# Linear attention and an MLP mixer in one kernel: the last batch's outputs sent in 16 transfers of two queues, not 24

## The chip, the core and the metric

The kernel runs on one core of a Trainium2 chip. The metric is the device time of one execution in microseconds (us); the time before is the median of three runs. One more execution was taken by the hardware profiler, and the profile's views come from it.

## The reference

For 8 batches, 8 heads of 64 columns and 576 rows (float32 in and out), the reference computes a linear attention and feeds it to a mixer:

```python
q_p, k_p = phi(q), phi(k)                      # phi(x) = elu(x) + 1
kv  = einsum('bhsd,bhse->bhde', k_p, v)
num = einsum('bhsd,bhde->bhse', q_p, kv)
den = einsum('bhsd,bhd->bhs', q_p, k_p.sum(axis=2))[..., None] + 1e-06
x   = (num / den), laid out as (8, 576, 512)
h   = relu(x.transpose(0, 2, 1) @ w_tok1) @ w_tok2   # 576 -> 256 -> 576, mixes the rows
u   = x + h.transpose(0, 2, 1)
out = u + relu(u @ w_ch1) @ w_ch2                    # 512 -> 1536 -> 512
```

## The kernel before

The 576 rows of a batch lie as 64 groups of 9. Eight of the nine rows of each group are packed in pairs into four row tiles of 128 partitions: in a tile, partitions 0 to 63 hold one row of each group and partitions 64 to 127 the next one. The ninth rows ("tails") of two batches share a tile of their own. Matmuls run in bf16, sums in float32 PSUM.

Every piece of work is a named step, registered with `put(name, function, arguments)`. The string `ORDER` is a hand-written list of step names, and the kernel issues the steps in exactly that order. Each engine and each queue works through its own part of the list in order, and a step waits on semaphores for the data that it needs. A name begins with the batch, so 7... is the last batch. The steps that matter here:

- `7p<i><j>` (`product`, L959), i = 1 to 7, j = 0 or 1: the seven products of a Strassen-Winograd scheme for the last matmul, `relu(...) @ w_ch2`, of the row tiles 2j and 2j+1. Each is six matmuls of 128x256 into a PSUM bank.
- `7R<i><j>` (`product_read`, L973): VectorE (DVE) adds product i to one 256-column half of a row tile in the float32 buffer `obuf`. Each half of a row tile gets two such additions; the one with the later place in `ORDER` completes it. Products 1 and 2 make tile d = 0, columns 0 to 255; 6 and 3 the same tile's columns 256 to 511; 5 and 7 tile d = 1, columns 256 to 511, with 4 for its columns 0 to 255, which build on the same bank.
- `7D<i><j><e>` (`product_put`, L978): a DMA of one finished column half of one partition half (e) of a row tile to HBM: 64 rows of 256 float32, 64 KB. It is sent by SyncE (SP) for e = 0 and by ScalarE (ACT) for e = 1. ScalarE has no computation left at that time.
- `7ta<i>`, `7tb<i>`, `7t<i>` (`tail_product`, L1012), `7tr<i>` (`tail_read`, L1019), `7td<i><b>` (`tail_put`, L1024): the same for the tails of batches 4 to 7, two tiles of 128 rows; again SP sends partitions 0 to 63 and ACT partitions 64 to 127.

So the last batch's output and the four tails leave in 2 (j) x 4 (halves of two tiles) x 2 (e) = 16 transfers of L978 and 4 x 2 = 8 of L1024, 12 on each of the two queues. The outputs of the earlier batches leave through GpSimd (POOL) (`pair_put`, L1062, two transfers of 512 KB a batch), and nothing else is sent in the last microseconds. The program has eight completion semaphores for the transfers of SP and ACT and uses them in turn, so a transfer also waits until the eighth before it has landed. After the last step SP waits for all transfers to land (L1180), and a barrier of all engines ends the program.

Of the kernel before, what the change touches and what calls it, by code (L numbers as in the profile page):

```python
# [16 lines left out]

NO = 6

GSW = {2: 0, 1: 1}  # L20

HOLD = {2: 'p0 p1 p2', 1: 's2 s3 s2'}
# [5 lines left out]
ON_DVE = {'1v0', '2v1', '0r3', '0r6', '0r9', '1r5', '1r8'}  # L28

ON_POOL = set()  # L30

BANK = {k_: int(v_) for k_, v_ in (e.split(":") for e in """2K:5 2n0:2 2n1:4 2n2:6 2f:2 2g0:5 2g1:2 2X2:7 2Z2:0 2Y2:2 2gt:6 3K:6 3n0:2 3n1:4 3n2:6 3f:3 3g0:2 3g1:4 3X2:1
3Z2:5 3Y2:6 3gt:6 4K:2 4n0:2 4n1:4 4n2:6 4f:4 4g0:3 4g1:6 4X2:1 4Z2:4 4Y2:3 4gt:6 5K:3 5n0:2 5n1:4 5n2:6 5f:5
# [61 lines left out]
7y02 7y06 6p70 7y16 7x07 7y15 6eW 7x22 7y21 7x25 6hW 7y22 6p41 7y25 7x17 7F4 W1 7x26 7c2 7s4 7y26 7y17 7x23  # L95
7cr2 7x03 7x14 7y03 7x27 7y14 7y23 6p40 7y07 7x13 7c0 7w30 6eX 7c3 7y27 6o 7x04 7x12 7y04 7x24 7y12 7cr0 7c4
7cr3 7y13 7y24 7p10 7w34 7cr4 7w12 7p11 7w10 7w22 7c1 7w14 7w24 7p50 7R10 7cr1 7w20 7c5 7w40 7w42 7p60 7w32
7cr5 7w44 7ta2 7ts1 7R60 7ta1 7tb1 7p70 7tr1 7R11 7p21 7ts2 7R50 7p61 7R21 7R70 7p30 7D701 7ts4 7tb2 7p40 7p20
7R40 7R30 7t6 7D401 7ts3 7tr2 7D300 7R61 7D211 7p51 7tr6 7D700 7R20 7D301 7t5 7td20 7R51 7D201 7p71 7D210 7tr5
7td21 7t7 7D200 7R71 7D400 7t3 7D711 7tr7 7D710 7p31 7td71 7tr3 7td70 7p41 7td31 7R31 7td30 7t4 7D311 7R41  # L100
7D310 7D411 7tr4 7D410 7td41 7td40"""


@with_exitstack
def kernel(
# [20 lines left out]
    nc = tc.nc  # L126

    B, H, S, D = q.shape
# [3 lines left out]
    R = 4  # L132
    R1 = R + 1
    T = 2 * R + 1
    TD = T * D
# [14 lines left out]
    def bank(name):  # L150
        return psum[:, BANK[name]]
# [11 lines left out]
    def const(name, shape, dt=BF16):  # L163
        return consts.tile(shape, dt, name=name, tag=name)
# [18 lines left out]
    ut = [const(f"ut{i}", [128, DM]) for i in range(2)]  # L183
    uT = [const(f"uT{b}", [128, R, NDM, 128]) for b in range(2)]
    uTj = [t.rearrange("p r j c -> p (r j c)").rearrange("p (j r c) -> p j r c", j=NDM, r=R) for t in uT]
    ebuf = [const(f"e{i}", [128, 2 * TD]) for i in range(4)]
    ybuf = [const(f"y{i}", [128, 2 * TD]) for i in range(2)]
    uTt = const("uTt", [128, 2, NDM, 128])
    cr = [const(f"cr{b}", [128, NCH, SM]) for b in range(2)]
    crt = const("crt", [128, NCH, 128])  # L190
    obuf = const("obuf", [128, NO, DM], FP32)
    swc = const("swc", [128, len(GSW), 4, 2, 256])

# [5 lines left out]
    half = [slice(0, 64), slice(64, 128)]  # L199
# [27 lines left out]
    def put(name, fn, *a):  # L227
        assert name not in tok, name
        tok[name] = lambda: fn(*a)
# [4 lines left out]
    def slots(name, m):  # L234
        return obuf[:, SLOT[name]:SLOT[name] + m]
# [120 lines left out]
            in0=v_[:, :, :, 0:D],  # L356
            in1=den[:, :, :, None].to_broadcast([128, m, HG, D]), op=ALU.mult)

    for i in range(3):
        for c in range(2):  # L360
            put(f"1n{i}{c}", nd1_mm, i, c)
            put(f"1nc{i}{c}", nd1_end, i, c)
# [49 lines left out]
            out=xv[:, :, 3, m], in0=nd_tile(n, m)[:, :, at, 0:D],  # L412
            in1=dens[:, m, :, at, None].to_broadcast([128, 2, D]), op=ALU.mult)

    for n in range(2, B):
        put(f"{n}n", nd_mm, n)
        put(f"{n}nd", nd_den, n)
        put(f"{n}ne", nd_last, n)
        for m in range(3):
            put(f"{n}n{m}", nd_six, n, m)  # L420
        for m in range(2):
            put(f"{n}o{m}", nd_one, n, m)
# [62 lines left out]
    for n in range(1, B):  # L485
        for mt in range(NT):
            put(f"{n}f{mt}", mm1, n, mt)
            put(f"{n}fr{mt}", mm1_read, n, mt)
        if n > 1:
            for i in range(2):  # L490
                put(f"{n}g{i}", mm2, n, i)
                put(f"{n}gu{i}", mm2_read, n, i)
                put(f"{n}uT{i}", utr_dma, n, i)
        if n > 1 and n % 2:
            put(f"{n}gt", mm2_tails, n // 2)
            for b in range(2):
                put(f"{n}gt{b}", mm2_tails_read, n // 2, b)
            put(f"{n}ut", utr_tail_dma, n // 2)
# [173 lines left out]
    def mm3(n, mc, kjs):  # L672
        b = n % 2
        for kj in kjs:
            nc.tensor.matmul(out=bank(f"{n}m{mc}"), lhsT=wc1[:, kj, 128 * mc:128 * mc + 128],  # L675
                             rhs=uTj[b][:, kj] if n < 2 else uT[b][:, :, kj],
                             start=(kj == 0), stop=(kj == NDM - 1))

    def mm3_read(n, mc):
# [6 lines left out]
    for n in range(B - 1):  # L686
        for mc in range(NCH):
            if n < 2:
                put(f"{n}ma{mc}", mm3, n, mc, range(0, 2))
                put(f"{n}mb{mc}", mm3, n, mc, range(2, NDM))  # L690
            else:
                put(f"{n}m{mc}", mm3, n, mc, range(NDM))
            put(f"{n}r{mc}", mm3_read, n, mc)
# [47 lines left out]
    outv = out.rearrange("n (p t) d -> n p t d", t=T)  # L741
# [76 lines left out]
    def ablock(n, i, e):  # L818
        return cr[n % 2].rearrange("p k (j e s) -> p k j e s", j=2, e=2)[:, KH * i:KH * (i + 1), :, e]
# [7 lines left out]
    def row_sums(n, which, k0, m):  # L827
        live["row", n, which, k0] = winograd(
            sb, [ablock(n, i, e) for e in range(2) for i in range(2)], which, slice(k0, k0 + m),
            nc.gpsimd if f"{n}w{which}{k0}" in ON_POOL else nc.vector)  # L830

# [15 lines left out]
    def cblock(m, h):  # L847
        return wc1[:, 2 * h:2 * h + 2, HM * m:HM * (m + 1)]
# [21 lines left out]
    def u_sums(n, which):  # L870
        t, b = tu if n == B - 1 else tuc, n % 2
        b11, b12, b21, b22 = [ublock(h, e, b) for h in range(2) for e in range(2)]
        x_, y_ = {1: (b12, b11), 2: (b22, t[0]), 3: (b22, b12), 4: (b21, t[1])}[which]
        (nc.gpsimd if f"{n}s{which}" in ON_POOL else nc.vector).tensor_tensor(
            out=t[which - 1], in0=x_, in1=y_, op=ALU.subtract)

    for n in range(2, B):
        for w in range(1, 5):
            put(f"{n}s{w}", u_sums, n, w)

    def group_sums(g, which):
        s_ = swc[:, GSW[g]]
        a11, a12, a21, a22 = [cblock(m, h)[:, :, 256 * g:256 * g + 256] for m in range(2) for h in range(2)]
        o, x_, y_, op = ((0, a21, a22, ALU.add), (1, s_[:, 0], a11, ALU.subtract),
                         (2, a11, a21, ALU.subtract), (3, a12, s_[:, 1], ALU.subtract))[which - 1]
        (nc.gpsimd if f"G{g}{which}" in ON_POOL else nc.vector).tensor_tensor(
            out=s_[:, o], in0=x_, in1=y_, op=op)

    for g in GSW:
        for w in range(1, 5):  # L890
# [11 lines left out]
    def mix_mm(n, g, i):  # L902
# [5 lines left out]
        else:  # L908
            s_, t, c0 = [swc[:, GSW[g], w] for w in range(4)], tuc, 0
        w_ = lambda m, h: cblock(m, h)[:, :, 256 * g:]  # L910
# [23 lines left out]
            o, c = {2: (dst(0, 0), c1), 3: (dst(0, 1), c6), 7: (dst(1, 1), c5)}[i]  # L934
            add_relu(o, ps, c)

    for n in range(2, B):
        for g in range(3) if n == B - 1 else GSW:
            for i in range(1, 8):
                put(f"{n}x{g}{i}", mix_mm, n, g, i)  # L940
                put(f"{n}y{g}{i}", mix_read, n, g, i)
# [21 lines left out]
    HC = [slice(0, 256), slice(256, 512)]  # L963
# [11 lines left out]
    def product_put(n, i, j, e):  # L975
        o = slots(f"{n}P{j}", 2)
        d, c = {2: (0, 0), 7: (1, 1), 3: (0, 1), 4: (1, 0)}[i]
        [nc.sync, nc.scalar][e].dma_start(out=outv[n, :, 2 * (2 * j + d) + e, HC[c]],  # L978
                                          in_=o[half[e], d, HC[c]])

    for n in range(1, B):
        for i in range(1, 8):
# [2 lines left out]
    for i in range(1, 8):  # L985
        for j in range(2):
            put(f"7R{i}{j}", product_read, 7, i, j)
            for e in range(2):
                if i in (2, 3, 4, 7):
                    put(f"7D{i}{j}{e}", product_put, 7, i, j, e)  # L990


# [28 lines left out]

    def tail_put(i, b):
        e, c = {2: (0, 0), 7: (1, 1), 3: (0, 1), 4: (1, 0)}[i]
        (nc.sync, nc.scalar)[b].dma_start(out=outv[B - 4 + 2 * e + b, :, 2 * R, HC[c]],  # L1024
                                          in_=slots("7t", 2)[half[b], e, HC[c]])

    for w in range(1, 5):
        put(f"7ts{w}", tail_sums, w)
    for i in range(1, 8):
        if i < 3:  # L1030
            put(f"7ta{i}", tail_product, i, range(KH - 1))
            put(f"7tb{i}", tail_product, i, range(KH - 1, KH))
        else:
            put(f"7t{i}", tail_product, i, range(KH))
        put(f"7tr{i}", tail_read, i)
        for b in range(2):
            if i in (2, 7, 3, 4):
                put(f"7td{i}{b}", tail_put, i, b)


# [144 lines left out]
```

## Time and profile before

| | |
|---|---|
| median of 3 runs | 248.88 us (248.19 to 249.03) |
| profiled execution | 248.42 us; span from first to last instruction 246.6 us; granted TensorE clock 0.997 |
| PE busy | 235.1 us (95%), 2538 matmuls |
| DVE busy | 204.1 us (83%) |
| ACT busy | 136.9 us (56%) |
| POOL busy | 78.7 us (32%) |
| output transfers of SP and ACT | 12 + 12 of 64.0 KB, 2.1 us to landing (median) |
| HBM read, written | 35.85 MB, 9.44 MB |

Engines are PE (TensorE matmul), DVE (VectorE), ACT (ScalarE), POOL (GpSimd) and SP (SyncE). An engine name with a q (ACTq, SPq) stands for its queue, and what it issues (a DMA) is not counted as busy time. L978 is line 978 of the kernel before. A DMA's duration in the timeline is that of its issue on the queue; the time to landing counts from the start of the issue until the last piece has arrived.

### The profile page before, as it was taken

What the parts mean: (1) busy time and instruction counts of PE and PEld (TensorE: products, weight loads), DVE (VectorE), ACT (ScalarE), POOL (GpSimd) and SP (SyncE); (2) the same over time, 40 slices, a digit from 0 to 9 for tenths busy, and PEclk for the clock granted to TensorE, in tenths of its full rate; (3) what the DMA queues carried; (4) which work ended last, traced back from release to release, by engine and by line L of the source; (5) the groups of instructions that cost most, each with busy time, mean ns of one, the idle gap of its engine ahead of it and who ended that gap; (6) DMA issues with size and microseconds to landing.
All of it is one profiled execution on the core that took longest, in us unless ns stands there. A gap on an engine that the chain in (4) does not pass through costs nothing.

```text
span 246.6 us, 6211 instructions
## 1 busy us (share of the span) xinstructions
PE 235.1 (95%) x2538; PEld 168.5 (68%) x2556; DVE 204.1 (83%) x368; ACT 136.9 (56%) x224; POOL 78.7 (32%) x88
## 2 busy tenths in 40 slices
PE   7899999999999999999999999999999999999990
PEld 3584445565776676777777676867687758888880
DVE  5954686999899899998996989889997789687670
ACT  4761882579684298429957378448822742535000
POOL 9770047071900440062000260044006700532730
PEclk9999999999999999999999999999999999999998
DMA  6999999988879996399939984599375434126145
GB/s 251 266 203 253 362 239 290 387 235 206 318 210 204 304 335 167 77 262 334 351 104 204 313 273 99 104 190 295 77 160 24 88 85 88 21 45 142 35 115 139
DMA packets 50445, 48.42 MB, mean 196 GB/s; under 512 B 30192, under 2 KB 36720, under 8 KB 50416
## 3 DMA queue, kind: packets, MB, share of 16 engines
q1 hardware_dynamic: 41984, 35.00, 49.9%
q0 software_dynamic: 7472, 12.22, 23.9%
q10 hardware_dynamic: 960, 0.79, 1.4%
q8 instruction: 20, 0.33, 0.5%
q14 instruction: 9, 0.07, 0.1%
HBM read 35.85 MB, written 9.44 MB: 184 GB/s over the span
## 4 chain that ended last, share of the span: by engine, by line
PE 88%; DVE 3%; DMA 3%; issue 2%; ACT 2%; DVEq 0%; SPq 0%; ACTq 0%
PE ps L959 24%; PE ps L917 16%; PE ps L675 15%; PE ps L437 6%; PE ps L736 6%; PE ps L448 4%; PE ps L700 2%; PE ps L722 2%; PE ps L291 2%; PE ps L1012 2%; PE ps L376 2%; DMA k_raw<-in_k_dram 2%; DMA qT<-qp 1%; PE ps L309 1%; PE ps L616 1%
## 5 line engine op out<-in xcount | busy, mean ns | idle before, releaser
L675 PE MATMUL ps<-uT,wc 128*128 128x512 bf16 x171 | 40.9, 379 | 0.2
L684 ACT ACTIVATE cr<-ps 128x512 bf16<-128x512 f32 x39 | 22.4, 600 | 23.3 <-PE ps L675 18.1
L1058 POOL TENSOR_TENSOR obuf<-obuf,q_raw 128x512 f32<-128x512 f32 x6 | 8.8, 1465 | 72.0 <-DVE obuf L1051 72.0
L959 PE MATMUL ps<-k_raw,v_raw 128*128 128x256 bf16 x252 | 31.6, 273 | 0.0
L675 PEld LDWEIGHTS <-wc 128*128 128x128 bf16 x176 | 16.7, 98 | 16.7 <-issue 0.2
L959 PEld LDWEIGHTS <-cr 128*128 128x128 bf16 x252 | 24.3, 98 | 5.0 <-issue 0.4
L959 PEld LDWEIGHTS <-v_raw 128*128 128x128 bf16 x252 | 24.3, 98 | 3.9 <-issue 0.4
L241 ACT ACTIVATE e<-q_raw 128x1152 bf16<-128x1152 f32 x16 | 18.7, 1168 | 8.6 <-DMA q_raw<-in_q_dram 8.3
L959 PE MATMUL ps<-wc,cr 128*128 128x256 bf16 x168 | 21.6, 273 | 0.1
L241 ACT ACTIVATE e<-k_raw 128x1152 bf16<-128x1152 f32 x16 | 18.6, 1167 | 2.4 <-DMA k_raw<-in_k_dram 2.3
L1051 DVE TENSOR_TENSOR obuf<-ps,u 128x512 f32<-128x512 f32 x24 | 16.3, 685 | 3.5 <-PE ps L959 2.2
L917 PEld LDWEIGHTS <-swc 128*128 128x128 bf16 x160 | 15.6, 98 | 3.5 <-issue 0.5
L917 PEld LDWEIGHTS <-wc 128*128 128x128 bf16 x156 | 15.1, 98 | 4.1
L402 DVE TENSOR_TENSOR x<-ps,dens 128x768 bf16<-128x768 f32 x18 | 16.8, 951 | 0.2
L917 PE MATMUL ps<-crt,swc 128*128 128x256 bf16 x120 | 15.5, 272 | 0.3 <-ACT q_raw L932 0.3
L251 DVE TENSOR_TENSOR kp<-e,y 128x1152 bf16<-128x1152 bf16 x16 | 11.9, 754 | 4.5 <-ACT e L241 4.3
L459 DVE TENSOR_TENSOR u<-ps,x 128x1024 bf16<-128x1024 f32 x12 | 14.6, 1220 | 1.0 <-PE ps L448 0.6
L825 DVE TENSOR_TENSOR v_raw<-cr 128x512 bf16<-128x512 bf16 (+3 forms) x24 | 14.6, 618 | 0.0
L1058 POOL TENSOR_TENSOR obuf<-obuf,w 128x512 f32<-128x512 f32 x6 | 7.8, 1294 | 21.0 <-DVE obuf L1051 21.0
L437 PE MATMUL ps<-x,w 128*128 128x512 bf16 x50 | 13.9, 379 | 0.4
L917 PE MATMUL ps<-uT,wc 128*128 128x256 bf16 x104 | 14.1, 273 | 0.0
L264 ACT CAST vs<-v_raw 128x1152 bf16<-128x1152 f32 x12 | 13.9, 1162 | 0.0
(168 smaller groups left out, 494.9 us busy)
## 6 DMA issues: line engine op xcount, KB each, us to landing
k_raw<-in_k_dram SPq DMA_DIRECT2D x16, 576.0 KB, 6.9
q_raw<-in_q_dram SPq DMA_DIRECT2D x16, 576.0 KB, 6.8
v_raw<-in_v_dram SPq DMA_DIRECT2D x14, 576.0 KB, 6.0
out_dram<-obuf POOLq DMA_DIRECT2D x12, 512.0 KB, 6.4
wc<-in_moe_w_ch_dram POOLq DMA_DIRECT2D x8, 384.0 KB, 10.1
out_dram<-obuf POOLq DMA_DIRECT2D x4, 256.0 KB, 3.5
out_dram<-obuf ACTq DMA_DIRECT2D x12, 64.0 KB, 2.1
out_dram<-obuf SPq DMA_DIRECT2D x12, 64.0 KB, 2.1
```

What stands on the lines that cost most here:

```text
L241: nc.scalar.activation(out=ebuf[EBUF[f"{n}{nm}{c}"]], in_=f, func=AF.Exp)
L402: nc.vector.tensor_tensor(out=xv[:, :, rc0:rc0 + 3], in0=nd_tile(n, m)[:, :, k0:k0 + 6, 0:D].rearrange("p i (q a) d -> p i q a d", a=2), i ...
L437: nc.tensor.matmul(out=banks(f"{n}f")[:, mt], lhsT=w1t[:, b, ms] if r == R else w1[:, r, ms], rhs=x[b][:, r, :], start=(r == 0), stop=(r = ...
L459: nc.vector.tensor_tensor(out=u[b][:, rs], in0=banks(f"{n}g{i}"), in1=x[b][:, rs], op=ALU.add)
L675: nc.tensor.matmul(out=bank(f"{n}m{mc}"), lhsT=wc1[:, kj, 128 * mc:128 * mc + 128], rhs=uTj[b][:, kj] if n < 2 else uT[b][:, :, kj], start ...
L684: nc.scalar.activation(out=o, in_=ps, func=AF.Relu)
L736: nc.tensor.matmul(out=bank(f"U{p}{t}"), lhsT=crt[:, kc, :] if t == 8 else cr[b][:, kc, 128 * r:128 * r + 128], rhs=wc2[:, kc, :], start=( ...
L825: return engine.tensor_tensor(out=s_[which - 1][:, ks], in0=x_, in1=y_, op=op)
L917: nc.tensor.matmul(out=ps[:, j], lhsT=lhs[:, k_, 128 * j:128 * (j + 1)], rhs=rhs[:, :, k_], start=(first and j == 0 and k_ == 0), stop=(k_ ...
L959: nc.tensor.matmul(out=ps, lhsT=lhs[:, k_], rhs=rhs[:, k_], start=(first and not skip and k_ == 0), stop=(k_ == KH - 1), skip_group_check= ...
L1051: nc.vector.tensor_tensor(out=slots(f"{n}P", 4)[:, d::2, HC[c]], in0=pair_tile(n, "X" if z == "W" else z), in1=u[n % 2][:, d::2, HC[c]], o ...
L1058: nc.gpsimd.tensor_tensor(out=o, in0=o, in1=part[i], op=ALU.add)
```

## The change

A wide transfer takes the place of two: where a row tile's two column halves were sent one after the other, all 512 columns are sent at once, after the half that is completed later. This is done for four of the (row tile, partition half) pairs, those with j = 0, and for both tail tiles. The row tiles with j = 1 keep their column halves. The steps 7D3.. and 7D4.. of j = 0 and the steps 7td3. and 7td4. go, and what is left stands at other places of `ORDER`: 7D70. now comes after 7R40, 7D20. after 7R30 and 7R20, 7td2. after 7tr3, and 7td7. is the last step, after 7tr4. In all, 8 transfers of 64 KB and 8 of 128 KB leave on the two queues. No other step of `ORDER` moves, and the instructions of PE, DVE and POOL are the same in the same order.

```diff
+WHOLE = {'00', '01', 't0', 't1'}
...
-7cr5 7w44 7ta2 7ts1 7R60 7ta1 7tb1 7p70 7tr1 7R11 7p21 7ts2 7R50 7p61 7R21 7R70 7p30 7D701 7ts4 7tb2 7p40 7p20
-7R40 7R30 7t6 7D401 7ts3 7tr2 7D300 7R61 7D211 7p51 7tr6 7D700 7R20 7D301 7t5 7td20 7R51 7D201 7p71 7D210 7tr5
-7td21 7t7 7D200 7R71 7D400 7t3 7D711 7tr7 7D710 7p31 7td71 7tr3 7td70 7p41 7td31 7R31 7td30 7t4 7D311 7R41
-7D310 7D411 7tr4 7D410 7td41 7td40"""
+7cr5 7w44 7ta2 7ts1 7R60 7ta1 7tb1 7p70 7tr1 7R11 7p21 7ts2 7R50 7p61 7R21 7R70 7p30 7ts4 7tb2 7p40 7p20 7R40
+7R30 7t6 7D701 7ts3 7tr2 7R61 7D211 7p51 7tr6 7R20 7t5 7R51 7D201 7p71 7D210 7tr5 7t7 7D200 7R71 7D700 7t3
+7D711 7tr7 7D710 7p31 7tr3 7p41 7td21 7R31 7td20 7t4 7D311 7R41 7D310 7D411 7tr4 7D410 7td71 7td70"""
...
     def product_put(n, i, j, e):
         o = slots(f"{n}P{j}", 2)
         d, c = {2: (0, 0), 7: (1, 1), 3: (0, 1), 4: (1, 0)}[i]
-        [nc.sync, nc.scalar][e].dma_start(out=outv[n, :, 2 * (2 * j + d) + e, HC[c]],
-                                          in_=o[half[e], d, HC[c]])
+        w = slice(0, 512) if f"{j}{d}" in WHOLE else HC[c]
+        [nc.sync, nc.scalar][e].dma_start(out=outv[n, :, 2 * (2 * j + d) + e, w],
+                                          in_=o[half[e], d, w])
...
-                if i in (2, 3, 4, 7):
+                if i in (2, 7) or i in (3, 4) and f"{j}{i - 3}" not in WHOLE:
                     put(f"7D{i}{j}{e}", product_put, 7, i, j, e)
...
     def tail_put(i, b):
         e, c = {2: (0, 0), 7: (1, 1), 3: (0, 1), 4: (1, 0)}[i]
-        (nc.sync, nc.scalar)[b].dma_start(out=outv[B - 4 + 2 * e + b, :, 2 * R, HC[c]],
-                                          in_=slots("7t", 2)[half[b], e, HC[c]])
+        w = slice(0, 512) if f"t{e}" in WHOLE else HC[c]
+        (nc.sync, nc.scalar)[b].dma_start(out=outv[B - 4 + 2 * e + b, :, 2 * R, w],
+                                          in_=slots("7t", 2)[half[b], e, w])
...
-            if i in (2, 7, 3, 4):
+            if i in (2, 7) or i in (3, 4) and f"t{i - 3}" not in WHOLE:
                 put(f"7td{i}{b}", tail_put, i, b)
```

The rest of the diff gives names to constants (`NE = 4`, `NY = 2`, `U1 = 0`) that keep their values, and registers steps of batch 1 that `ORDER` doesn't name; neither issues an instruction.

More of the change, by code (lines that the diff above doesn't have):

```diff
@@ L18 @@
 NO = 6
+NE = 4
+NY = 2
+U1 = 0
 GSW = {2: 0, 1: 1}
@@ L185 @@
     uTj = [t.rearrange("p r j c -> p (r j c)").rearrange("p (j r c) -> p j r c", j=NDM, r=R) for t in uT]
-    ebuf = [const(f"e{i}", [128, 2 * TD]) for i in range(4)]
-    ybuf = [const(f"y{i}", [128, 2 * TD]) for i in range(2)]
+    ebuf = [const(f"e{i}", [128, 2 * TD]) for i in range(NE)]
+    ybuf = [const(f"y{i}", [128, 2 * TD]) for i in range(NY)]
     uTt = const("uTt", [128, 2, NDM, 128])
@@ L357, in nd1_end @@
             in1=den[:, :, :, None].to_broadcast([128, m, HG, D]), op=ALU.mult)
-    for i in range(3):
+    for i in range(0 if U1 == 2 else 3):
         for c in range(2):
@@ L413, in nd_one @@
             in1=dens[:, m, :, at, None].to_broadcast([128, 2, D]), op=ALU.mult)
-    for n in range(2, B):
+    for n in range(2 - U1, B):
         put(f"{n}n", nd_mm, n)
@@ L488 @@
             put(f"{n}fr{mt}", mm1_read, n, mt)
-        if n > 1:
+        if n > 1 or U1:
             for i in range(2):
@@ L675, in mm3 @@
             nc.tensor.matmul(out=bank(f"{n}m{mc}"), lhsT=wc1[:, kj, 128 * mc:128 * mc + 128],
-                             rhs=uTj[b][:, kj] if n < 2 else uT[b][:, :, kj],
+                             rhs=uTj[b][:, kj] if n < 2 - U1 else uT[b][:, :, kj],
                              start=(kj == 0), stop=(kj == NDM - 1))
@@ L875, in u_sums @@
             out=t[which - 1], in0=x_, in1=y_, op=ALU.subtract)
-    for n in range(2, B):
+    for n in range(1, B):
         for w in range(1, 5):
@@ L935, in mix_read @@
             add_relu(o, ps, c)
-    for n in range(2, B):
+    for n in range(1, B):
         for g in range(3) if n == B - 1 else GSW:
```

## The prediction

> **What bounds the kernel now.** I read the page first: PE is busy 95% of the span and carries 88% of the chain, so time is won in matmuls or where PE has already stopped. The last digit of its row, 0, says that PE has stopped there. The end of the chain of waits tells when:
>
> ```profile
> 238.61 1.31 PE ps L959 x12
> 239.92 0.67 PE ps L1012 x6
> 240.59 0.02 issue
> 240.61 0.42 DVE obuf L1019
> ```
>
> The last matmul ends at 240.59, the last addition (step 7tr4) at 240.61 + 0.42 = 241.03. The span is 246.6, so 5.6 us follow in which no engine computes. The timeline of that stretch:
>
> ```profile
> 240.35 1.15 ACTq L1024 DMA_DIRECT2D out_dram<-obuf  x2
> 240.41 1.41 SPq L1024 DMA_DIRECT2D out_dram<-obuf  x2
> 240.61 0.42 DVE L1019 TENSOR_TENSOR obuf<-ps,ut 128x256 f32<-128x256 f32 x1 [0.23 <-PE ps L1012]
> 241.59 1.20 ACTq L978 DMA_DIRECT2D out_dram<-obuf  x2
> 241.92 1.19 SPq L978 DMA_DIRECT2D out_dram<-obuf  x2
> 242.88 0.55 ACTq L1024 DMA_DIRECT2D out_dram<-obuf  x1
> 243.20 0.55 SPq L1024 DMA_DIRECT2D out_dram<-obuf  x1
> ```
>
> SP's last transfer, 7td40, starts at 243.20 although its data stood ready at 241.03: 2.17 us late. The two transfers ahead of it begin at 241.92 and take 1.19 together, and the next starts 1.28 after them: 0.64 us for each (0.55 of issue, the rest a wait on a semaphore). The queue is not waiting for data any more, it is working off a list. Its transfers from 242.8 on land so:
>
> ```profile
> L1024 SPq DMA_DIRECT2D out_dram<-obuf x1: 550/550/550, 243.2 to 243.2; - x1
> DMA to landing us min/median/max: 2.0/2.0/2.0
> ```
>
> So the last landing is 243.20 + 2.0 = 245.20, and 1.4 us of closing waits and barriers follow to 246.6. Those 1.4 stay.
>
> An earlier place shows where part of the lag began: the transfers issued from 236.3 to 238, and the queues from 236 to 239.
>
> ```profile
> L978 ACTq DMA_DIRECT2D out_dram<-obuf x2: 582/1284/1985, 235.7 to 236.4; - x2
> L978 SPq DMA_DIRECT2D out_dram<-obuf x1: 1668/1668/1668, 236.7 to 236.7; - x1
> DMA to landing us min/median/max: 3.2/3.6/3.7
> ...
> q8 instruction: 1, 0.02, 3.3%
> ```
>
> One load of instructions holds one of the 16 DMA engines for 3.3% of 16 x 3 us = 1.6 us; beside it one issue on each queue takes 1.99 and 1.67 us in place of 0.55, and both end at about 238.4. That costs each queue some 1.1 to 1.4 us.
>
> Last, the windows, which show whether the DMA engines could go faster (the last two columns are their busy share and GB/s; the first line is batch 6's output, which POOL sends, one half of the partitions after the other):
>
> ```profile
> 225.00:228.00 3.00, 3.00 (x30) 2.67 (x29) 2.96 (x9) 1.51 (x3) 0.00 (x0) 1.00 0.96 202
> 239.20:239.40 0.20, 0.20 (x4) 0.18 (x2) 0.10 (x1) 0.00 (x0) 0.00 (x0) 1.00 0.89 184
> 239.40:239.60 0.20, 0.20 (x4) 0.18 (x3) 0.20 (x1) 0.00 (x0) 0.00 (x0) 1.00 0.95 308
> 239.80:244.60 4.80, 0.77 (x8) 0.44 (x5) 0.85 (x2) 0.00 (x0) 0.00 (x0) 1.00 0.84 198
> 241.60:242.00 0.40, 0.00 (x0) 0.00 (x0) 0.00 (x0) 0.00 (x0) 0.00 (x0) 1.00 0.94 236
> ```
>
> Divided by the share: 210 GB/s at full occupation for POOL's, 207, 324, 236 and 251. So the tail is close to a second limit: 0.84 of the DMA engines' time is taken while two queues send 64 KB each 0.64 us. Fewer issues therefore do not buy their whole 2.17 us.
>
> **Part by part.** *What is removed:* eight of 24 issues, four on each queue. At 0.64 each this is 2.6 us of list per queue. *What is added:* each of the eight remaining wide transfers carries 128 KB, in 64 rows of 2 KB instead of 1 KB. The bytes are the same, 24 x 64 = 1536 KB. PE, DVE and POOL run the same instructions in the same order with the same waits, so 241.03 for the last addition stays. *What is moved:* a wide transfer waits for the later of its two halves. On DVE's times (an addition takes 0.42; the transfers follow within 0.04), ACT now starts 7D701 at 234.52 (after 7R40), 7D211 at 235.1, 7D201 at 236.17 (after 7R20), 7D711 at 237.8, 7td21 at 239.1 (after 7tr3), 7D311 at 239.76, 7D411 at 240.42, 7td71 at 241.07. SP starts 7D210 already at 232.5, then 7D200 at 236.17, 7D700 at 236.8, 7D710 at 237.8 and the same last four steps as ACT. The gaps from 7td2 on are 0.65, as wide as 0.64 per issue, so no list builds up there: the last issue starts when its data are ready, at 241.07 and not 243.20. The first gain is 2.13.
>
> The load of instructions at 236.45 belongs to a stream that is not changed (q8 moves 20 loads in the run, and PE's instructions stay), so I leave it there. Before, it struck two queues that had no slack. Now the third transfer behind it is 7D711 or 7D710; held to 238.4 it is 0.05 to 0.6 late, and both queues then wait for 7tr3 until 239.1. Cover: that wait. Each issue also waits for the landing of the eighth transfer before it (the program uses eight completion semaphores in turn): for the last pair these are 7D710 and 7D711, issued by 238.4 at the latest and landed at 238.4 + 2.0 = 240.4, ahead of 241.03. Cost nothing; without that cover, the 3.7 us that the slowest of the delayed transfers took to land would make it 237.8 + 3.7 = 241.5, or 0.4 lost.
>
> *What is given back:* the data of the end. From 7td2 on, 256 + 128 + 128 + 256 = 768 KB (786 kB) must go, and the last 256 KB become ready together. A landing of 2.0 for 64 KB (65.5 kB, 0.28 at the tail's 236) leaves 1.7 that does not depend on size. The DMA engines are taken as one server: it starts with 7td2's pair at 239.1 and ends at the later of 239.1 + 786/rate and 241.07 + 262/rate, and 1.7 later all has landed. At 207 GB/s, the single-queue rows: 242.90, landing 244.60, gain 0.60. At 324, the best window: 2.43 gives 241.53, but the last pair needs 241.07 + 0.81 = 241.88; landing 243.58, gain 1.62. At 240, between the two-queue rows 236 and 251: 3.28, so 242.38, landing 244.08, gain 1.12. I take 240: after the change SP's lower half and ACT's upper half always stand ready together, which is what those rows show. No row has 2 KB rows of output; POOL's larger pieces at 210 and the 1 KB rows at 207 bound it below, and neither is faster for its size.
>
> A rule speaks against this. The Trainium skill, page "DMA: Bandwidth & Descriptors", section "Rules for kernel authors", says that two transfers to disjoint partition halves are not worth making, because they share the same engines and serialize. Taken strictly it would put the pairs at the single-half rate, a gain of 0.6 instead of 1.1. The windows at 0.94 and 0.95 share are above that, so I follow the rows. The same page, section "Issuing engines are not separate DMA queues", calls the sequencer's issue time usually small beside the transfer, by which eight issues fewer would be worth nothing; here an issue's 0.55 is longer than its 0.28 of data.
>
> *Sum:* the profiled execution took 248.42 (span 246.6 and 1.82 around it); 248.42 - 1.12 = 247.30. It lies 0.46 under the median of the three runs, 248.88, and from the median the forecast is 248.88 - 1.12 = 247.76, so 247.8.
>
> **The rivals.** *The forecast, list gone, data rate the new limit:* 248.88 - 1.62 to 248.88 - 0.76, i.e. 247.3 to 248.1. For it: 2.17 us of lag in plain sight, after PE's end. 0.70. A measurement here tells 0.3%, or 0.75 us, from no change; the gain passes 0.75 if the rate is above 215 GB/s (786/215 = 3.66; landing 244.46).
>
> *No difference that shows:* the halves go one after the other at 202 to 210, and the DMA engine that was held brings a rest into the end. At 207 the gain is 0.60, less the 0.4 of the cover above if it fails: 0.2 to 0.6, so 248.3 to 248.7. For it: the share of 0.84, and POOL's 4 KB pieces being no faster. Against: two rows over 230 with both queues at work. 0.25. Here also falls that the change does not do what it says, if the two queues had not been the limit and only the data rate; then 24 or 16 issues are the same, within 0.3 of 248.9.
>
> *Slower:* a load of instructions falls on the last pair. ACT and SP run shorter programs, so their own loads (q14, 9 in the run) can move; if one as long as the 1.6 us of 236.45 starts when the last pair's data do, one DMA engine is held with its share of the pair, and the pair takes what the slowest of the delayed transfers took, 3.7 from the issue, and up to the 262/207 = 1.27 of its own, larger data besides. 241.07 + 3.7 + 1.27 = 246.04, which is 0.84 later than 245.20: 249.72. It decides only if the load is long and begins within about 1 us of 242.3. Against: the q14 loads carry half of q8's bytes. 0.05.
>
> **How the numbers follow.** Likeliest 247.8. The range must hold 8 in 10: below, the gain of 1.62 and 0.3 for the scatter of the runs (248.19 to 249.03) give 246.9 to 247.0; above, the no-difference case from 0.2 of gain, 248.7. Faster 0.70, same 0.25, slower 0.05.
>
> **What would show it.** Right: 16 issues of the two queues, eight of 128 KB; the last two start within 0.1 us of each other at the end of the last addition; between 239 and the end no issue waits behind another; the last landing some 2.5 to 3.3 us after its issue instead of 2.0; the closing 1.4 unchanged. A DMA share near 0.95 with about 210 GB/s to the end would show the second case. Wrong: an addition of L973 or L1019 later against PE than now, an issue of over 1 us after 239, or a last landing after 245.2.

## The result and the profile after

| | before | after |
|---|---|---|
| median | 248.69 us (248.19 to 250.44, 8 runs) | 247.34 us (246.59 to 247.96, 8 runs) |
| ratio, 95% interval | | 0.9938 (0.9912 to 0.9964) |
| profiled execution | 248.42 us, span 246.6 us | 247.27 us, span 245.5 us |
| end of the last addition | 241.03 us | 241.69 us |
| last landing after that | 4.17 us | 2.77 us |
| from the last landing to the end | 1.36 us | 1.04 us |
| SP's last landing after the last addition | 4.17 us | 2.45 us |
| from SP's last landing to the end | 1.36 us | 1.36 us |

The change is faster by 1.35 us in the medians, 1.5 us by the ratio; the interval reaches from 0.9 to 2.2 us. The end of the chain of waits after (start, us, what):

```profile
240.57 0.67 PE ps L1020 x6
241.24 0.02 issue
241.27 0.42 DVE obuf L1027
```

The lines are numbered anew: L1020 was L1012, L1027 was L1019, L1033 was L1024, L986 was L978. The last addition ends at 241.27 + 0.42 = 241.69, which is 0.66 later than before. The moved transfers are not the cause: the same addition of batch 1 already shows it, long ahead of any instruction that was moved. Before, on DVE's timeline:

```profile
45.41 0.42 DVE L353 TENSOR_TENSOR x<-ps,den 128x256 bf16<-128x256 f32 x1
```

and after:

```profile
46.14 0.42 DVE L360 TENSOR_TENSOR x<-ps,den 128x256 bf16<-128x256 f32 x1
```

Up to here 0.73 are lost, of which 0.07 come back later. Another early instruction of DVE, the same one in every kernel, stood anywhere between 43.3 and 44.6 us in the profiles of this study, in no order of kernels. So single profiled executions are compared here by their tail, the time from the end of the last addition to the end of the span: 5.53 us before, 3.81 after, a gain of 1.72, which the 0.66 brings down to the 1.1 that the two spans differ by.

The timeline of the tail after:

```profile
239.75 0.47 SPq L1033 DMA_DIRECT2D out_dram<-obuf  x1
239.76 0.50 ACTq L1033 DMA_DIRECT2D out_dram<-obuf  x1
...
240.41 1.12 SPq L986 DMA_DIRECT2D out_dram<-obuf  x2
240.41 1.58 ACTq L986 DMA_DIRECT2D out_dram<-obuf  x2
...
241.27 0.42 DVE L1027 TENSOR_TENSOR obuf<-ps,ut 128x256 f32<-128x256 f32 x1 [0.23 <-PE ps L1020]
241.72 0.47 SPq L1033 DMA_DIRECT2D out_dram<-obuf  x1
242.09 0.56 ACTq L1033 DMA_DIRECT2D out_dram<-obuf  x1
```

SP's last transfer starts 0.03 after the last addition, where it was 2.17. ACT's starts 0.40 after it: the two issues before it took from 240.41 to 241.99 together, 1.58 where SP took 1.12. The transfers from 241.6 on land so:

```profile
L986 ACTq DMA_DIRECT2D out_dram<-obuf x1: 474/474/474, 241.5 to 241.5; - x1
L1033 SPq DMA_DIRECT2D out_dram<-obuf x1: 467/467/467, 241.7 to 241.7; - x1
L1033 ACTq DMA_DIRECT2D out_dram<-obuf x1: 563/563/563, 242.1 to 242.1; - x1
...
DMA to landing us min/median/max: 2.2/2.4/2.4
```

The two L1033 take 2.42 (SP) and 2.37 (ACT), so they land 2.45 and 2.77 after the last addition. It is SP's landing that sets the end, not the later one of ACT. After its last issue SP waits for the transfers to land, and it waits once, before (first line) and after (second line):

```profile
SPq L1180 <- DMA out_dram<-obuf: 1.4, 1, 1.4
```

```profile
SPq L1189 <- DMA out_dram<-obuf: 1.9, 1, 1.9
```

Before, this wait runs from 243.82 to 245.20, the landing of 7td40. After, it runs from 242.26 to 244.14, the landing of SP's own 7td70, while ACT's 7td71 lands only at 244.46. SP looks at the completion semaphores one after the other, 0.06 us each. The one of its last transfer is the first of the eight output semaphores that it looks at, and 7td71's is the last. SP comes to that one 2.89 after the last addition, 0.12 after 7td71 has landed, and has no need to wait there. The time from SP's last landing to the end is 1.36 in both kernels.

The load of instructions falls at the same place in the work as before (it begins 4.64 ahead of the last addition, before 4.58), as the queues from 236 to 239 and SP's issues at that time show:

```profile
q8 instruction: 1, 0.02, 1.9%
```

```profile
L986 SPq DMA_DIRECT2D out_dram<-obuf x2: 467/741/1015, 236.8 to 237.3; - x2
```

It was shorter this time (1.9% of 16 x 3 us, 0.9 us), one of SP's issues took 1.0 us, and at 239.75 both queues started on time. The 1.57 us that this load took in the profile of the kernel before is the longest of the 14 profiles; in the others it took 0.88 to 1.30.

### The profile page after: what moved, and what is told of

It is laid out like the page before. It is cut to its first block, busy times and chain, and to the rows that moved or that the text cites. A ratio compares the mean times of both kernels' runs of the same rounds, so it can differ in the third digit from the quotient of the medians.

```text
span 245.5 us, 6217 instructions
## 1 busy us (share of the span) xinstructions
PE 235.7 (96%) x2556; PEld 168.1 (68%) x2556; DVE 204.2 (83%) x368; ACT 136.8 (56%) x224; POOL 78.5 (32%) x88
## 4 chain that ended last, share of the span: by engine, by line
PE 81%; DMA 12%; POOL 2%; DVE 1%; issue 1%; ACT 1%; DVEq 0%; SPq 0%; POOLq 0%; ACTq 0%
PE ps L966 24%; PE ps L924 16%; PE ps L682 11%; DMA wc<-in_moe_w_ch_dram 7%; PE ps L444 6%; PE ps L743 6%; PE ps L455 4%; DMA cr<-in_v_dram 3%; PE ps L707 2%; PE ps L729 2%; PE ps L298 2%; PE ps L1020 2%; PE ps L383 2%; DMA qT<-qp 1%; POOL qT L1107 1%
## 5 line engine op out<-in xcount | busy, mean ns | idle before, releaser
L682 PE MATMUL ps<-uT,wc 128*128 128x512 bf16 x176 | 41.6, 379 | 0.1
L444 PE MATMUL ps<-x,w 128*128 128x512 bf16 x56 | 14.4, 379 | 0.0
```

Source lines behind the costliest of these rows:

```text
L444: nc.tensor.matmul(out=banks(f"{n}f")[:, mt], lhsT=w1t[:, b, ms] if r == R else w1[:, r, ms], rhs=x[b][:, r, :], start=(r == 0), stop=(r = ...
```

## The experiments

Tails below are from the end of the last addition to the end of the span, and "lands" is the last landing after that addition; both come from one profile of each kernel. A transfer is late by the time from the last addition to the start of its issue, and a list is the issues that stand in a queue. The expectations call the length of the lists theory 1, with the data rate as the next limit. Rival 2 is that the load of instructions is the whole lateness, rival 3 that rows of 2 KB go faster than rows of 1 KB.

**e1 and e2: the load of instructions moved out of the outputs.** The same edit in the kernel before (e1) and in the changed one (e2):

```diff
+    def fill(m):
+        z = zeros.bitcast(BF16)
+        for _ in range(m):
+            nc.tensor.matmul(out=bank("warm0")[:, 0:128], lhsT=z[:, 0:128], rhs=z[:, 128:256],
+                             start=True, stop=True)
...
-lambda: warm(0, 4),
+lambda: (warm(0, 2), fill(32)),
```

> The kernel before, with 60-odd cheap PE instructions more in the warm-up at the start (two of the four warming matmuls become 32 small ones), so that PE's load of instructions that fell at 236.45, into the output transfers, falls some 3 us earlier, ahead of their data. Measure: the tail, from the end of the last addition to the end of the span, 5.57 us before and 3.81 after; and the median. Theory 1, the lists of issues alone: 12 issues of 0.64 us per queue are the limit with or without the load; what the load cost (1.1 to 1.4 us per queue) comes off, but 12 x 0.64 = 7.7 us from 234.8 still end at about 242.5 with landing and closing: tail 4.3 to 4.7, median 0.8 to 1.3 us faster than before. Rival 2, the load is the whole lag: tail as after, 3.6 to 3.9, and e2 equal to it. Rival 3, row size (2 KB rows go faster): nothing changes here, tail 5.3 to 5.6.

> The changed kernel with the same shift of PE's load of instructions. Theory 1: the load lay under slack already, tail 3.5 to 3.8, median within 0.3 us of the changed kernel (1.3 to 1.7 us faster than before). Rival 2: the same as e1, within 0.2 us. Rival 3: as the changed kernel, 3.8.

| | median | ratio | tail | lands |
|---|---|---|---|---|
| e1 (24 transfers, load moved) | 248.23 | 0.9984 (0.9959 to 1.0008) | 4.46 | 3.11 |
| e2 (16 transfers, load moved) | 247.90 | 0.9956 (0.9930 to 0.9982) | 3.80 | 2.75 |

The end of e1's timeline, and the landings of its output transfers:

```profile
241.92 0.42 DVE L1019 TENSOR_TENSOR obuf<-ps,ut 128x256 f32<-128x256 f32 x1 [0.23 <-PE ps L1012]
242.16 1.20 SPq L978 DMA_DIRECT2D out_dram<-obuf  x2
242.51 0.55 ACTq L1024 DMA_DIRECT2D out_dram<-obuf  x1
243.45 0.55 SPq L1024 DMA_DIRECT2D out_dram<-obuf  x1
```

```profile
DMA to landing us min/median/max: 2.0/2.0/2.3
```

The load now fell 8.1 us ahead of the last addition, and no issue is held any more. The list of 12 still ends 243.45 - 242.34 = 1.11 late, where it was 2.17. So of the 1.72 of tail, 1.07 was the load on lists without slack, and 0.66 the length of the lists by itself; in the changed kernel moving the load brings nothing (3.80 for 3.81). The 0.66 is SP's last landing, 3.11 after the last addition in e1 and 2.45 in e2: it is issued 1.08 earlier and takes 0.42 longer to land. Theory 1 stands, and its rival "the load alone" falls by the 0.66. The medians moved less than expected, and e1's is not clearly different from before. The early DVE instruction stood at 44.6 us in both; that the altered warm-up put the later work back is not shown, since it stood at 44.6 in e12 too, with the old warm-up.

**e3 and e4: half the bytes, the same issues.**

```diff
+    HQ = [slice(0, 128), slice(256, 384)]
...
-        ... HC[c] ...           # in product_put and tail_put, 64 KB
+        ... HQ[c] ...           # 32 KB; the wide ones of e4: slice(0, 256)
```

> The kernel before with all its 24 transfers, each sending only 128 of its 256 columns (half of the last outputs is left out): 32 KB, the same number of issues. Theory 1: the lists stay as long, only the last landing is 0.1 to 0.2 us shorter: tail 5.2 to 5.5, median within 0.4 us of before. Rival 3, and any theory in which the data rate set the end before: half the bytes free the engines, tail 4.2 or less, median 1.3 us faster.

> The changed kernel with half the columns in every transfer (64 KB and 32 KB; half of the last outputs is left out): the 16 issues stay, half the data. Theory 1 with the data rate as the new limit: the last two start at the end of the last addition and land after 2.0 us, not 2.4 to 2.8: tail 3.1 to 3.4, median 0.4 to 0.7 us below the changed kernel. If the issues still set the end: tail 3.6 to 3.8, median as the changed kernel.

e3: median 248.06, ratio 0.9979 (0.9946 to 1.0011), tail 5.04, lands 3.68; SP's last issue starts 1.82 late, not 2.16. The load was shorter in this run (1.19 for 1.57 us), and the issue that it held took 1.33 for 1.67, 0.34 less. The other 0.15 of the 0.49 is the shorter landing (1.85 for 2.00). Halving the data leaves the lists as they were: the kernel before was limited by issues. e4 is inconclusive: median 246.63, ratio 0.9919 (0.9889 to 0.9948), but the tail of its profile is 3.94, not 3.1 to 3.4. A load of instructions of 0.65 us began 1.18 after the last addition and SP's last 64 KB took 2.57 to land; besides, with only the first columns read, 7td2 no longer waited for 7tr3 and went out earlier.

**e5: the gap between ACT's issues.**

```diff
     nc.scalar.activation(out=one, in_=one, func=AF.Exp)
+    for _ in range(6):
+        nc.scalar.copy(out=one, in_=one)
```

> The changed kernel with six tiny ScalarE copies more at the start, nothing else. In the changed kernel's trace ACT's last transfer started 0.40 us after the last addition and SP's 0.03; ACT had lost 0.35 between two issues. In before the same gap lies between other transfers, but at the same place of ACT's instruction stream: between its 319th and 320th instruction. Theory 1a: crossing that place costs ACT some 0.35 us; six instructions more move it ahead of 7D711, where ACT waits anyhow: the last two transfers start within 0.1 us of the last addition, tail 3.4 to 3.7 in place of 3.81. Theory 1b, the gap comes from the transfers themselves (a full queue): it stays, tail 3.8. The median tells no more than 0.3 us here.

Median 246.71, ratio 0.9936 (0.9914 to 0.9957), tail 3.80, lands 2.76.

```profile
240.47 0.42 DVE L1027 TENSOR_TENSOR obuf<-ps,ut 128x256 f32<-128x256 f32 x1 [0.23 <-PE ps L1020]
240.92 0.47 SPq L1033 DMA_DIRECT2D out_dram<-obuf  x1
241.12 0.55 ACTq L1033 DMA_DIRECT2D out_dram<-obuf  x1
```

The gap left the end: the last pair starts 0.03 and 0.23 late instead of 0.03 and 0.40. The last landing did not move at all, 2.76 for 2.77, and SP's, which sets the end, stayed too (2.44 for 2.45). So ACT's late start cost nothing. This misses the 3.4 to 3.7 that was expected, though the gap moved as theory 1a said.

**e6, e7, e8: which transfers are wide.** 20, 18 and 12 transfers; `ORDER` places each transfer after the addition that completes it.

```diff
-WHOLE = {'00', '01', 't0', 't1'}
+WHOLE = {'00', '01'}                              # e6: the tails in halves
+WHOLE = {'00', '01', 't0'}                        # e7: the second tail tile in halves
+WHOLE = {'00', '01', '10', '11', 't0', 't1'}      # e8: all wide
```

> Only the row tiles with j = 0 wide (WHOLE = 00, 01); the tails go in halves as before, each half placed right after the addition that completes it: 20 transfers, 10 per queue. Theory 1 (issues and slack): from 7D71 on each queue has an issue every 0.64 us and data every 0.65, so nothing piles up unless the load of instructions does it; the last transfer is 64 KB again. Tail 3.4 to 3.8, the same as the changed kernel or up to 0.4 better. If row size (2 KB) were what helped, the tails' part of the gain is lost: tail 4.3 or more.

> As the changed kernel, but the second tail tile in halves (WHOLE = 00, 01, t0): 7td7 goes out after 7tr7 and 7td4 after the last addition, 64 KB each: 18 transfers. The last pair carries 128 KB in place of 256 and 128 KB leave 2.6 us earlier. Theory 1 with the data rate as the new limit: the last landing is 0.3 to 0.5 us earlier than in the changed kernel, tail 3.3 to 3.6. If data do not matter at the end: tail 3.7 to 3.9.

> All row tiles and tails wide: 12 transfers of 128 KB, six per queue, the same bytes. The last four pairs (7td2, 7D2, 7D7, 7td7) are then 1024 KB in 2 us. Theory 1 with the data rate as the new limit: 1049 kB at 260 to 270 GB/s from 1.93 us before the last addition end 2.0 us after it, plus 1.7: landing 3.7, tail 4.7 to 5.0, median about 1 us slower than the changed kernel. Fewer issues alone: tail 3.8 or less, no slower than the changed kernel. At 324 GB/s or more, as in the best window: tail 4.0 to 4.2.

| | transfers | median | ratio | SP's, ACT's last start after the last addition | lands | tail |
|---|---|---|---|---|---|---|
| e6 | 20 | 247.19 | 0.9945 (0.9924 to 0.9966) | 0.99, 0.48 | 2.98 | 4.08 |
| e7 | 18 | 247.30 | 0.9935 (0.9913 to 0.9957) | 0.46, 0.21 | 2.55 | 3.77 |
| after | 16 | 247.34 | 0.9938 (0.9912 to 0.9964) | 0.03, 0.40 | 2.77 | 3.81 |
| e8 | 12 | 247.94 | 0.9971 (0.9950 to 0.9991) | 0.03, 0.25 | 3.60 | 4.76 |

Fewer issues are better only down to a point. With 20 and 18 transfers the lists still run late, and both miss what was expected: 0.64 per issue against 0.65 per addition leaves next to no slack to make up for the load of instructions. e7's tail, 3.77, lies where its expectation put it "if data do not matter at the end"; its last landing did come 0.22 sooner, but SP's came 0.10 later than the changed kernel's, and the end followed it after 1.23 in place of 1.36, since another semaphore was the last to be reached. With 12 SP is on time, and the last 1 MB is ready too late. The medians tell 12 from 18 and 20 (0.6 to 0.8 us, runs of one chip); they do not tell 16, 18 and 20 apart. e8's landings from 241.3 on, and the window of its last data:

```profile
DMA to landing us min/median/max: 3.0/3.3/3.5
```

```profile
241.20:245.00 3.80, 0.15 (x2) 0.00 (x0) 0.42 (x1) 0.00 (x0) 0.00 (x0) 1.00 0.85 269
```

From the start of 7td2, 1.93 before the last addition, 1049 kB landed by 3.60 after it; without the 1.7 that every landing takes, that is 3.83 us, 274 GB/s. The same sum for the changed kernel, whose window reads

```profile
241.00:243.90 2.90, 0.23 (x3) 0.00 (x0) 0.46 (x2) 0.00 (x0) 0.00 (x0) 0.99 0.91 257
```

is 786 kB in 1.93 + 2.77 - 1.7 = 3.0 us, 262 GB/s. Two kernels with different sizes at the end give one rate, within 5%. This rests on the estimate of 1.7: the windows that hold all the packets of these data, of the changed kernel and of e8, read

```profile
240.80:244.10 3.30, 0.43 (x4) 0.14 (x2) 0.66 (x2) 0.00 (x0) 0.00 (x0) 0.96 0.85 241
```

```profile
240.90:244.90 4.00, 0.45 (x5) 0.16 (x2) 0.69 (x2) 0.00 (x0) 0.00 (x0) 1.00 0.85 264
```

so the packets moved at 241 and 264 GB/s, an 8 KB load of instructions in each included.

**e9 and e10: a third queue.**

```diff
-        (nc.sync, nc.scalar)[b].dma_start(...)                                   # e9, on top of e7
+        (nc.gpsimd if i == 7 else (nc.sync, nc.scalar)[b]).dma_start(...)
...
-        [nc.sync, nc.scalar][e].dma_start(...)                                   # e10, in the kernel before
+        (nc.gpsimd if f"{i}{j}" in ('20', '21', '40') else [nc.sync, nc.scalar][e]).dma_start(...)
```

In e10, 7D401 stands beside 7D400 in `ORDER`, so that it comes after POOL's sums.

> The changed kernel with the second tail tile in halves, as in the run with 18 transfers, but the early half (7td7, two transfers of 64 KB) goes through POOL's queue, which is idle by then. There SP's list had run late by 0.46 us because of the added issue. Theory 1: SP and ACT have the changed kernel's slack again, the last pair carries 128 KB: last landing 2.2 to 2.4 us after the last addition, tail 3.4 to 3.6. If POOL's transfers get in the way on the DMA engines, or the data rate alone sets the end: tail 3.7 or more.

> The kernel before with its 24 transfers of 64 KB in 1 KB rows, but six of them (7D20, 7D21 and 7D40 of both halves) sent by POOL, which is idle after its last sums: 9 issues on each of SP and ACT. Theory 1 (number of issues per queue): the lists of SP and ACT shrink by 1.9 us each, last landing 2.1 to 2.8 us after the last addition, tail 3.5 to 4.1, nearly all of the change's gain with 1 KB rows. Rival 3 (row size, or the total number of transfers): tail 5.2 or more.

e10: median 247.43, ratio 0.9962 (0.9942 to 0.9982), tail 4.25, lands 3.03. 24 transfers of 64 KB in 1 KB rows bring 1.28 of the 1.72 (1.13 by SP's last landing, 0.15 by the order of the looks); what helped is the number of issues per queue, not the size of the rows. It fell 0.15 short of the range, since SP's last issue still started 0.99 after the last addition:

```profile
241.30 0.42 DVE L1019 TENSOR_TENSOR obuf<-ps,ut 128x256 f32<-128x256 f32 x1 [0.23 <-PE ps L1012]
242.52 0.47 ACTq L1024 DMA_DIRECT2D out_dram<-obuf  x1
242.72 0.47 SPq L1024 DMA_DIRECT2D out_dram<-obuf  x1
```

e9: median 247.23, ratio 0.9954 (0.9934 to 0.9973), tail 4.23, lands 3.04: a miss. SP's lists had their slack back (last start 0.03 late), but POOL's two transfers went to the same DMA engines as the pairs behind them, whose landings rose to as much as 3.2 us; SP's last landing came at 2.87, not 2.45. The bytes from 7td2 on, with POOL's, are the changed kernel's 786 kB, and the sum above, 1.93 + 3.04 - 1.7, gives 240 GB/s here and not 262: it does not hold for every order of sending.

**e11: the order of the closing looks.**

```diff
+    nc.scalar.dma_start(out=const("spare", [128, 1], FP32), in_=moe_w_tok1[0:128, 0:1])
```

> The changed kernel with one tiny load (512 bytes) on ACT's queue at the start, which turns the eight completion semaphores on by one: 7td71 then lands on the one that SP looks at second at the end, 7td70 on the third; in the changed kernel 7td71's is the last one looked at. Theory 1d: SP looks at the semaphores one after the other, 0.06 us each, so the seven looks that come after the last landing put the closing time from 1.04 to 1.30 to 1.40 us; tail 4.0 to 4.2 in place of 3.81. If the order of the looks costs nothing: closing 1.0 to 1.1, tail 3.8.

Median 247.40, ratio 0.9964 (0.9946 to 0.9981), tail 4.14. The last landing is as in the changed kernel, 2.79 after the last addition, but 1.35 and not 1.04 follow: as expected. SP's one wait is now for ACT's 7td71:

```profile
SPq L1190 <- DMA out_dram<-obuf: 2.2, 1, 2.2
```

It runs from 0.57 to 2.79 after the last addition. The transfers are the same, and their landings nearly so; the tail is 0.33 longer by the order of the looks alone.

**e12: a shorter end.** On top of e7's `WHOLE` and order, 7D700 right behind 7D701, and e5's six copies:

```diff
-7R30 7t6 7D701 7ts3 ...  7R71 7D700 7t3
+7R30 7t6 7D701 7D700 7ts3 ...  7R71 7t3
```

> Three edits on the changed kernel: the second tail tile in halves (as with 18 transfers), 7D700 placed right after 7D701, ahead of 7D200 on SP's queue, which was idle there, so that one wide transfer fewer stands behind the load of instructions, and the six tiny ScalarE copies at the start. Theory 1: SP no longer runs late at the end (0.46 us with 18 transfers), the last two transfers start within 0.2 us of the last addition and carry 128 KB together, 2.1 to 2.4 us to landing: last landing 2.2 to 2.5 us after the last addition in place of 2.77, closing 1.2 to 1.35 because the last landing is not on the semaphore looked at last; tail 3.4 to 3.8, median at or up to 0.4 us below the changed kernel. If the data rate alone sets the end: last landing 2.7 or later, tail 3.9 or more.

Median 246.62, ratio 0.9911 (0.9880 to 0.9942), the lowest median of the study; its interval overlaps the changed kernel's, so that it beats that one is not shown. In its profile it lands at 2.57, the closing takes 1.30, and the tail is 3.87, just over what was expected; the lists still ran 0.23 and 0.51 late.

## Why the prediction was right

The forecast was 1.12 us of gain and the list as its cause; measured were 1.35 to 1.5 with an interval of 0.9 to 2.2, which does not tell 1.12 from the 1.72 of the tail. The 1.72 may be on the high side, as the profile before had the longest load of instructions; e3, with a load of 1.19, had 0.34 less lateness. Step by step:

- *The list.* Eight issues fewer put SP's last start from 2.17 to 0.03 after the last addition, as said: the first gain of 2.13 was right. ACT's start at 0.40 was not foreseen: an issue of 0.73 and a pause of 0.32 stood ahead of it, so the sign "no issue waits behind another" failed on that queue. By e5 it cost nothing. e3 (half the data, lateness as far as the load allows) and e10 (1 KB rows, fewer issues per queue) confirm the cause.
- *The load of instructions.* The prediction left it in place and said that the wait for 7tr3 covers it. e2 shows that cover whole: 3.80 and 3.81. e1 adds what was not worked out: of the old lateness, 1.1 was the load, so the change is worth 0.66 of tail where no load falls into the outputs.
- *What is given back, the term that was mis-sized.* The prediction's sum gives back 2.13 - 1.12 = 1.01; it was 0.42, as SP's last transfer took 2.42 to land in place of 2.00. This was below the 2.5 to 3.3 that the prediction named. Nearly all of it is the size of the transfer itself: 7D701, 128 KB sent with little beside it, took 2.38. The sum took all data from 7td2 on as one line before the last landing. That describes ACT's 7td71, for which it gave 3.05 after the last addition at 240 GB/s; 2.77 was measured, with packets at 241, so what was too large is the fixed 1.7: from the start of 7td2 to the last landing are 4.71, and less the 3.3 of packets about 1.4 are left. And SP's half went ahead of ACT's, and SP's landing, at 2.45, set the end.
- *The closing.* "Those 1.4 stay" holds for the landing that SP waits for, 1.36 before and after; after the last landing it was 1.04, since SP was by then at its looks. 2.13 - 0.42 + 0 is the 1.72 of the tail, within rounding.
- *The rivals.* "No difference" needed 207 GB/s for all data. The slower case, a load on the last pair, could be watched: a load of 8 KB (0.41 us) began 0.66 after the last addition of the changed kernel, and in e5, where it had moved ahead by 3.2 us, the last landing was the same, so a short one costs nothing there. In e4 one of 0.65 us stood beside a landing of 2.57 for 64 KB; one as long as 1.6 in that place did not occur.

One reading needs its rows by queue. The Trainium skill's rule for disjoint halves (page "DMA: Bandwidth & Descriptors", section "Rules for kernel authors") says that they serialize. The last pair agrees: from 243.1 to 243.3 nearly all the DMA engines' time is SP's queue (q1), from 243.7 to 243.9 it is ACT's (q10).

```profile
q1 hardware_dynamic: 25, 0.05, 104.0%
q10 hardware_dynamic: 6, 0.00, 4.7%
```

```profile
q10 hardware_dynamic: 35, 0.07, 99.4%
q1 hardware_dynamic: 3, 0.00, 0.8%
```

The prediction read the rule, taken strictly, as 207 GB/s for both halves, and went by its rows instead. The halves do follow one another, but not both at that rate: the windows within SP's half and within ACT's read 220 and 348 GB/s, and all the data moved at 241.

```profile
243.10:243.50 0.40, 0.00 (x0) 0.00 (x0) 0.00 (x0) 0.00 (x0) 0.00 (x0) 1.00 1.01 220
243.70:243.90 0.20, 0.00 (x0) 0.00 (x0) 0.00 (x0) 0.00 (x0) 0.00 (x0) 0.91 1.00 348
```
The prediction's rows from 239.20 and 239.40 were such halves too: SP's queue has 84.2% of the first, ACT's 82.0% of the second. Why the second half is faster was not settled.

## What to carry to other kernels

At the end of a kernel, compare the pace of the issues on each queue (here 0.64 us) with the pace at which results come (0.65) and with the data time of one piece (0.25 for 64 KB at 262 GB/s): a list with no slack turns any hold-up of a DMA engine into lateness up to the end. Merge the transfers that are ready early, keep those that are ready last small, and stop merging where the data that become ready last need longer than the issues that were saved: here 24 lost by issues and 12 by data, and 16, 18 and 20 can't be told apart by their medians. Find the landing that the end waits for; it need not be the last one, and the order in which the semaphores are looked at decides (0.33 us in e11). Single profiles are compared from the last common instruction, not by their spans.

## What the runs showed that I had not expected

- ACT stood still for 0.32 us at a fixed place of its instruction stream, between its 319th and 320th instruction, in the kernel before and in the changed one; six instructions more at the start moved it away from the end (e5). What ACT does there was not settled.
- A load of instructions on one DMA engine (16 KB for PE, 0.9 to 1.6 us) held an issue on SP's queue, and in the kernel before on ACT's too: 1.0 to 2.0 us in place of 0.55. With the load moved ahead (e1) no issue was held.
- The closing took 1.04 to 1.36 us after the last landing, by which of the completion semaphores got it.
